# A recurrent attention kernel: token AV in front of memory AV in shared accumulators, side work in one accumulator with ACT casts, the left projection spread over three steps

## The chip, the cores and the metric

The kernel runs on one core of a Trainium2 chip. The core has five engines with queues of their own: TensorE (PE; PEld in the profile is its weight loads), VectorE (DVE), ScalarE (ACT), GpSimd (POOL) and SyncE (SP, which issues DMAs here). They meet only at semaphores. The metric is device time in microseconds (us), lower is better, as the median of several runs.

## The reference

Two branches are mixed by a gate. Branch A is attention over segments of 32 tokens, one after the other, with 8 memory rows that are carried from segment to segment:

```python
for s in range(n_seg):                       # 64 segments of 32 tokens
    h = concat([mem, xs])                    # 8 memory rows + 32 tokens
    q, k, v = h @ Wq, h @ Wk, h @ Wv         # 32 heads of 128
    p = softmax(where(mask, q @ k.T * scale, -1e9))
    o = (p @ v) @ Wo                         # summed over heads
    mem = o[:, :M, :]                        # memory of the next segment
    outs.append(o[:, M:, :])
a = concat(outs)
b = gelu(layernorm(x) @ w1 + b1) @ w2 + b2
return g * a + (1 - g) * b                   # g = sigmoid((x * gate_w).sum(-1))
```

The sequence has 2048 tokens of width 512; everything is bf16. The mask lets every row see the memory, and a token see itself and earlier tokens. Only the memory rows make a recurrence: the outputs of the tokens of a segment are needed by nobody but the result.

## The kernel before

It first computes branch B and the gates (a PE-filled stage of some 100 us), then 64 steps, one per segment, then a tail.

A **step** works on 32 columns: 8 memory rows and the first 24 tokens of the segment. The 8 tokens that are left over in each segment (the "left" part) are projected for four segments at once, one **tile** of 128 tokens ahead, as side work. Wo of the left tokens, and the output rows, are side work too.

In order of TensorE, a step is this (line numbers of the profile). The projections to Q and K fill five PSUM banks (`qk_unit`, L211); DVE transposes each from its bank to SBUF as f32 (`qk_tr`, L217), and ACT, for one bank POOL, casts it to bf16 (L667). V follows in two banks (`v_unit`, L222), cast by ACT. Then come the scores (L383, and L387 for the left keys), Exp on ACT (L685, L686), and the sums of the memory queries by matmul (`sums`, L360). DVE takes their reciprocal (L692) and multiplies (Pm, L695). **Memory AV** (`av`, L398 and L403 with Pm) multiplies V by the probabilities of the 8 memory queries into four banks, one per group j of heads. Four copies bring them to UTT (L703), two on DVE and two on ACT, alternating. The sums of the token queries follow and DVE takes their large reciprocal (L704). Wo over all heads (`wo_unit`, L233) yields the 8 new memory rows and, in the same 32 columns, 24 token rows of an earlier segment. ACT casts the result (wsb, L711). `mask_mm` (L374) writes the mask into the score bank of the next step, the bank that the large reciprocal has read. **Token AV** (`av_x`: `av` with Px, the probabilities of the token queries) follows, for the segment before. `mem_out` (L365) transposes the new memory rows by matmul, and DVE copies them to hT (L721), for which the next step's first matmul waits.

Between these pieces the program pulls **units** of side work out of a generator (`run_fill`, `side_work`): four matmuls of 512 columns each, in most of them. Five units stand in the wait for Pm (six in the fourth step of a tile), one behind the sums, none (two in the fourth step) behind token AV, and what is left of the step's units at the end, behind `mem_out`. The first step of a tile holds 8 units of the left V, the second and third 8 units of left Q and K each, and the fourth two of `out_units` and eight of `wo_left`.

Side work accumulates in two banks, 5 and 6, in turn (`side`). What empties a bank is put into a queue of the program (`later`) and written out at set places: `flush(dve_q)` for transposes and output, `flush(act_q)` for the casts of V and of Wo's left rows. `side` itself flushes when the bank that it needs has not been emptied. POOL casts the transposed left Q and K (L264, L268), copies the left V from a DMA bounce into VL (L299), fills the token columns of hT, and computes Px and a running check sum (L620 to L622).

The order on each engine is the program's order (a manual schedule); waits are set between the pieces where one reads what another wrote or reuses a buffer. PSUM has eight banks: five rotate through the projections and the two AVs (`ring`), 5 and 6 serve the side work, 7 the scores. The tail (L725 to L789) finishes the last two segments, their Wo, and the last two tiles of output; a check of overflow (L796 to L805) follows, with a slow path that is not taken here.

Of the kernel before, what the change touches and what calls it, by code (L numbers as in the profile page):

```python
# [23 lines left out]
def kernel(ctx, tc, A_x, A_mem0, A_Wq, A_Wk, A_Wv, A_Wo, A_seg_len, B_x, B_w1, B_b1, B_w2, B_b2, gate_w, out):  # L24
    nc = tc.nc
    P = 128
# [147 lines left out]

    pools.update(nTt=2, nside=1)

# [17 lines left out]
    def side(shape, dtype=FP32):  # L194
        side_n[0] += 1
        n = pools["nside"]
        while side_n[0] - n in side_todo:
            flush(dve_q)
            flush(act_q)
        return bank(5 + side_n[0] % n, shape, dtype)  # L200

# [51 lines left out]
    def left_qk(T, t, hf):  # L253
        h0, h1 = HF[hf]
        bk = side([P, 512])
        side_k = side_n[0]
        for kc in range(KC):
            qk_unit(bk, GLs[T], t, h0, h1, kc)
            if kc < KC - 1:
                yield  # L260
        def ev():
            Tv = qk_tr(bk, h0, h1)
            if t == 0:
                nc.gpsimd.tensor_copy(out=QL[T % 2][:, h0:h1, :], in_=Tv)  # L264
            else:
                for hh in range(h0 // 8, h1 // 8):
                    r0 = 8 * hh - h0
                    nc.gpsimd.tensor_copy(out=KL[T % 2][:, :, :, hh, :], in_=Tv[:, r0:r0 + 8, :].rearrange("p g (s c) -> p g s c", c=LEFT))  # L268
        later(dve_q, ev, side_k)
        yield  # L270

    def left_v(T, vb):
# [7 lines left out]
        def ev():  # L280
            vt = pools["sb"].tile([P, 4, Dh], BF16, tag="vt", bufs=1, name="vt")
            nc.scalar.copy(out=vt[:].rearrange("p i e -> p (i e)"), in_=bk[:])
            if vb == 0:
                vds[T] = dr.tile([P, 4, 2, Dh], BF16, tag="vd", name="vd")
            nc.sync.dma_start(vds[T][:, 2 * vb:2 * vb + 2], vt[:].rearrange("p (a g) e -> p a g e", g=2))
            if vb == 1:
                src = vds.pop(T)[:].rearrange("(j s c) h g e -> j h c s (g e)", j=4, s=SPT)
                vs = pools["sb"].tile([P, SPT, 2, Dh], BF16, tag="vs", bufs=1, name="vs")
                for j in range(4):
                    for hh in range(4):  # L290
                        r0 = 32 * j + LEFT * hh
                        nc.sync.dma_start(vs[r0:r0 + LEFT].rearrange("p s g e -> p s (g e)"), src[j, hh])
                vls[T] = vs
# [7 lines left out]
    def wo_left(T):  # L301
        bk = side([P, Dm])
        side_k = side_n[0]
        for u in range(8):
            wo_unit(bk, UTT[T % 2], 32, u)
            if u < 7:
                yield

        def ev():
            w = cw.tile([P, Dm], BF16, tag="wsbL", bufs=1, name="wsbL")  # L310
            nc.scalar.copy(out=w[:], in_=bk[:])
            wsbLs[T] = w
        later(act_q, ev, side_k)
        yield

    def out_units(T):
        ob = side([P, Dm])
# [9 lines left out]
        def ev():  # L327
            o_sb = cw.tile([P, Dm], BF16, tag="o", bufs=1, name="o")
            nc.vector.scalar_tensor_tensor(out=o_sb[:], in0=ob[:], scalar=g_all[:, T:T + 1], in1=c_all[:, T, :], op0=ALU.mult, op1=ALU.add)
            nc.sync.dma_start(out2[T * P:(T + 1) * P, :], o_sb[:])  # L330
        later(dve_q, ev, side_k)
        yield

    def side_work(T, si):


        if si < 3 and T + 1 < NT:
            for n in range(2):
                if si == 0:
                    yield from left_v(T + 1, n)  # L340
                else:
                    yield from left_qk(T + 1, n, si - 1)
        if si == 3 and T >= 2:
            yield from out_units(T - 2)
        if si == 3 and T >= 1:
            yield from wo_left(T - 1)

# [43 lines left out]

    def av(U, n, s, V, Pt, c_main, c_left, u0):

        T, si = divmod(s, SPT)
        for i in range(NG):
            for j in range(4):
                q = slice(32 * j, 32 * j + 32)
                nc.tensor.matmul(U[j][:, i, :], lhsT=V[q, i, :], rhs=Pt[q, i, c_main:c_main + n],  # L398
                                 start=(i == 0), stop=False, skip_group_check=True, tile_position=(32 * j, 0))
        for g in range(2):  # L400
# [97 lines left out]
    def setup():  # L498
# [14 lines left out]
        for hf in range(2):  # L513
            for t in range(2):
                for _ in left_qk(0, t, hf):
                    pass
                flush(dve_q)
                yield
# [77 lines left out]
    cw = loop.enter_context(tc.tile_pool(name="cw", bufs=2))  # L596
    pools.update(ps=pb, sb=cw, nTt=3, nside=2)

# [31 lines left out]
    def ux_out(s):  # L630
        T, si = divmod(s, SPT)
        c0 = 24 - 8 * si
        for j, U in enumerate(Uxs.pop(s)):
            nc.scalar.copy(out=UTT[T % 2][:, :, j, c0 + M:c0 + 40], in_=U[:])  # L634

    for s in range(nseg):
# [14 lines left out]
        if s >= 2:  # L651
            ux_out(s - 2)
            flush(act_q)
        if s + 1 < nseg:
# [35 lines left out]
        nc.scalar.copy(out=v_out(V, 1), in_=vb1[:])  # L690
        run_fill(5 + (si == 3))
        nc.vector.reciprocal(out=R[:, 0:8 * NG].rearrange("p (i q) -> p i q", q=8), in_=sm[:])  # L692
        Pm = cw.tile([P, NG, 16], BF16, tag="Pm", bufs=1, name="Pm")
        for c in (8, 0):
            nc.vector.tensor_tensor(out=Pm[:, :, c:c + 8], in0=E[:, :, c:c + 8], in1=R[:, 0:8 * NG].rearrange("p (i q) -> p i q", q=8), op=ALU.mult)  # L695
        Um = [bank(k, [P, NG, 8]) for k in (nd, ne, na, nc_)]
        av(Um, 8, s, V, Pm, 8, 0, 0)
        sr = B[:, 0:NG * 32].rearrange("p (i q) -> p i q", q=32)
# [3 lines left out]
        for j in range(4):  # L702
            (nc.scalar.copy if j % 2 else nc.vector.tensor_copy)(out=UTT[Tp % 2][:, :, j, 24 - 8 * sp:24 - 8 * sp + M], in_=Um[j][:])  # L703
        nc.vector.reciprocal(out=R[:, 8 * NG:].rearrange("p (i q) -> p i q", q=32), in_=sr)  # L704
# [9 lines left out]
        S_next = mask_mm()  # L714
        if s >= 1:
            av_x(s - 1, (nd, ne, na, nc_))
        run_fill(2 * (si == 3))
        if s + 1 < nseg:
# [17 lines left out]
    nc.vector.tensor_tensor(out=Px[:, :, 32:40], in0=E[:, :, 48:56], in1=Rq[:, :, 24:32], op=ALU.mult)  # L736
    nc.gpsimd.tensor_tensor(out=racc[:, 8 * NG:], in0=racc[:, 8 * NG:], in1=Rl, op=ALU.add)
    Es.pop(s), Rs.pop(s)
    Pxs[s] = Px
    for _ in fill:  # L740
        pass
    flush(act_q, 9)

    def wo_x(sw, k, ut, c0):
        wp = bank(k, [P, Dm])
        for u in range(8):
            wo_unit(wp, ut, c0, u)
        wsb = cw.tile([P, Dm], BF16, tag="wsb", bufs=9, name="wsb")
        nc.scalar.copy(out=wsb[:], in_=wp[:])
        wsbs[sw + 2] = wsb  # L750

    U1, U0 = UTT[(NT - 1) % 2], UTT[NT % 2]
    wo_x(s - 2, nb, U1, 16)
    for j, U in enumerate(Uxs.pop(s - 1)):
        (nc.vector.tensor_copy if j % 2 else nc.scalar.copy)(out=U1[:, :, j, 8 + M:48], in_=U[:])
    for _ in out_units(NT - 2):
        flush(dve_q, 9)
    av_x(s, (nd, ne, na, nc_))
    wo_x(s - 1, nb, U1, 8)

# [3 lines left out]
    for j, U in enumerate(Ul):  # L764
        (nc.vector.tensor_copy if j % 2 else nc.scalar.copy)(out=U1[:, :, j, 32:40], in_=U[:, :, RIDE:32])
    wo_x(s, 6, U0, 0)
    T = NT - 1
# [155 lines left out]
```

## Time and profile before

| what | us |
|---|---|
| median of 10 runs (822.4 to 823.99) | 823.18 |
| the profiled execution | 822.21 |
| its span, first to last instruction | 820.4 |
| first matmul of the first step | 100.91 |
| first matmul of the last step | 795.91 |
| DVE busy | 493.2 |
| ACT busy | 446.1 |
| POOL busy | 272.3 |

The granted TensorE clock was 0.999 over the span. Times of rows are microseconds from the span's start, then the duration of the row; a row of the timeline merges several instructions of one kind (x32). In brackets stands how long the engine was idle before the row, and what ended that. The busy time of PE counts matmuls by modelled ends, so a busy PE may still wait. The lines themselves stand with the prediction.

### The profile page before, as it was taken

The page shows a single profiled execution, that of the slowest core. Times are in us where ns is not written, and L with a number is a line of the kernel's source. Part 1 is how long each engine was busy: PE and PEld are TensorE (multiplying, and loading weights), DVE is VectorE, ACT ScalarE, POOL GpSimd, SP SyncE. Part 2 cuts the span into 40 slices and gives each one's busy share as a digit, 9 for nine tenths or more (in the row PEclk, how much of TensorE's full clock was granted, in tenths as well). Part 3 has the DMA queues.
Part 4 walks back from the last instruction along what each step waited for, and adds up shares of the span by engine and source line. Part 5 has one row for each costly group of instructions (what it writes and reads, how often), then busy time and mean ns, then how long its engine had stood idle before and what let it go on. Part 6 is the DMA issues. An engine that isn't in the chain of part 4 may idle for free.

```text
span 820.4 us, 48425 instructions
## 1 busy us (share of the span) xinstructions
PE 792.5 (97%) x22001; PEld 444.2 (54%) x22013; DVE 493.2 (60%) x1022; ACT 446.1 (54%) x1239; POOL 272.3 (33%) x624
## 2 busy tenths in 40 slices
PE   6999999999999999999999999999999999999986
PEld 3666545555555555555555555555555555555543
DVE  5764256565656666665666565666566565756554
ACT  3555445555555555555555645555564555565553
POOL 8100224242434243243424242433333242424220
PEclk9999999999999999999999999999999999999999
DMA  8791300000000010101010100001010101010000
GB/s 305 245 405 51 104 28 12 25 16 17 24 20 26 13 34 10 37 11 35 5 38 9 31 16 21 25 18 28 10 36 11 36 4 40 7 33 8 10 5 24
DMA packets 38357, 37.59 MB, mean 46 GB/s; under 512 B 13561, under 2 KB 36578, under 8 KB 36610
## 3 DMA queue, kind: packets, MB, share of 16 engines
q1 hardware_dynamic: 38018, 34.31, 12.6%
q8 instruction: 174, 2.85, 1.4%
q0 software_dynamic: 128, 0.13, 0.1%
q14 instruction: 37, 0.30, 0.1%
HBM read 26.03 MB, written 6.29 MB: 39 GB/s over the span
## 4 chain that ended last, share of the span: by engine, by line
PE 93%; DVE 3%; DMA 1%; issue 1%; SPq 1%; ACT 1%; DVEq 0%; ACTq 0%
PE b L211 34%; PE b L233 18%; PE b L222 16%; PE b L398 5%; PE hp L470 4%; PE bp L487 4%; PE b L360 3%; PE b L374 2%; PE b L383 2%; PE b L365 2%; PE b L403 1%; DMA Wo_sb<-in_A_x_dram 1%; PE b L387 0%; DVE hT L721 0%; DVE Tt L217 0%
## 5 line engine op out<-in xcount | busy, mean ns | idle before, releaser
L217 DVE STREAM_TRANSPOSE Tt<-b 128x512 f32<-128x512 f32 (+1 forms) x384 | 225.7, 613 | 82.1 <-PE b L211 70.3
L211 PEld LDWEIGHTS <-hT 128*32 128x32 bf16 x5120 | 131.6, 97 | 108.1 <-DVE hT L721 23.9
L233 PE MATMUL b<-Wo_sb,UTT 128*32 128x512 bf16 (+1 forms) x2656 | 160.9, 378 | 1.3 <-ACT UTT L763 0.9
L222 PE MATMUL b<-Wv_sb,hT 128*32 128x512 bf16 x2048 | 141.9, 379 | 0.0
L211 PE MATMUL b<-Wq_sb,hT 128*32 128x512 bf16 x2048 | 133.4, 380 | 3.2 <-DVE hT L721 1.7
L211 PE MATMUL b<-Wk_sb,hT 128*32 128x256 bf16 (+1 forms) x3072 | 133.4, 308 | 0.0
L667 ACT CAST KT<-Tt 128x256 bf16<-128x256 f32 (+1 forms) x192 | 87.1, 476 | 53.6 <-DVE Tt L217 53.5
L620 POOL TENSOR_TENSOR Px<-E,R 128x256 bf16<-128x256 bf16 x63 | 42.4, 674 | 209.1 <-DVE R L704 209.1
L704 DVE RECIPROCAL R<-b 128x256 f32<-128x256 f32 x63 | 110.7, 1757 | 0.0
L667 POOL CAST QT<-Tt 128x512 bf16<-128x512 f32 x64 | 39.1, 611 | 187.2 <-DVE Tt L217 187.2
L233 PEld LDWEIGHTS <-UTT 128*32 128x32 bf16 x2656 | 64.6, 96 | 63.6 <-DVE UTT L703 12.1
L711 ACT CAST wsb<-b 128x512 bf16<-128x512 f32 x63 | 36.9, 585 | 111.2 <-PE b L233 111.2
L692 DVE RECIPROCAL R<-b 128x64 f32<-128x64 f32 x63 | 35.1, 557 | 78.5 <-PE b L360 78.5
L634 ACT CAST UTT<-b 128x256 bf16<-128x256 f32 x248 | 74.4, 387 | 9.9 <-PE b L403 7.6
L667 ACT CAST QT<-Tt 128x512 bf16<-128x512 f32 x64 | 39.6, 619 | 68.3 <-DVE Tt L217 68.3
L222 PEld LDWEIGHTS <-hT 128*32 128x32 bf16 x2048 | 49.6, 96 | 21.1
L475 ACT ACTIVATE hg<-hp,b_sb 128x256 bf16<-128x256 f32 x80 | 37.8, 473 | 40.3 <-PE hp L470 40.3
L398 PEld LDWEIGHTS <-V 32*128 32x128 bf16 x4064 | 34.5, 91 | 45.5 <-DVE Pm L695 32.2
L721 DVE CAST hT<-b 128x32 bf16<-128x32 f32 x63 | 12.1, 192 | 78.1 <-PE b L365 78.1
L470 PE MATMUL hp<-yT,w_sb 128*128 128x256 bf16 (+1 forms) x352 | 54.9, 282 | 2.3 <-DMA w_sb<-in_B_w_dram 1.1
L703 ACT CAST UTT<-b 128x64 bf16<-128x64 f32 x126 | 20.6, 215 | 66.1 <-PE b L403 66.1
L622 POOL TENSOR_TENSOR racc<-racc,R 128x320 f32<-128x320 f32 x63 | 54.7, 868 | 0.0
(131 smaller groups left out, 1053.9 us busy)
## 6 DMA issues: line engine op xcount, KB each, us to landing
Wv_sb<-in_A_Wv_dram SPq DMA_DIRECT2D x4, 1024.0 KB
Wq_sb<-in_A_Wq_dram SPq DMA_DIRECT2D x4, 1024.0 KB
Wk_sb<-in_A_Wk_dram SPq DMA_DIRECT2D x4, 1024.0 KB
Wo_sb<-in_A_Wo_dram SPq DMA_DIRECT2D x2, 2048.0 KB
vd<-vt SPq DMA_DIRECT2D x32, 128.0 KB
vs<-vd SPq DMA_DIRECT2D x256, 16.0 KB
out_dram<-o SPq DMA_DIRECT2D x15, 128.0 KB
Wo_sb<-in_A_x_dram SPq DMA_DIRECT2D x1, 1024.0 KB
```

Of the source, the lines that this page charges most:

```text
L211: nc.tensor.matmul(bk[32 * j:32 * j + 32, 0:n], lhsT=G[:, kc, :], rhs=W5[t][:, kc, h0:h1, j, :], start=(kc == 0), stop=(kc == KC - 1), til ...
L217: nc.vector.transpose(out=Tt[:, 0:n], in_=bk[:, 0:n])
L222: nc.tensor.matmul(bk[32 * j:32 * j + 32, :], lhsT=G[:, kc, :], rhs=Wv5[:, kc, 4 * vb:4 * vb + 4, j, :], start=(kc == 0), stop=(kc == KC - ...
L233: nc.tensor.matmul(bk[32 * g:32 * g + 32, :], lhsT=ut[:, i, j, c0:c0 + 32], rhs=Wo_sb[:, 4 * i + j, d0:d1], start=(j == 0 and i < 4), stop ...
L398: nc.tensor.matmul(U[j][:, i, :], lhsT=V[q, i, :], rhs=Pt[q, i, c_main:c_main + n], start=(i == 0), stop=False, skip_group_check=True, til ...
L470: nc.tensor.matmul(hp[:rows, :], lhsT=w1_sb[:, kc, fc * P:fc * P + rows], rhs=yTs[blk][:, kc, :], start=(kc == 0), stop=(kc == KC - 1))
L475: nc.scalar.activation(out=hg_[:rows, :], in_=hp[:rows, :], func=ACTF.Gelu_apprx_tanh, bias=b1_sb[:rows, fc:fc + 1], scale=1.0)
L620: nc.gpsimd.tensor_tensor(out=Px[:, :, 0:32], in0=E[:, :, 16:48], in1=Rr, op=ALU.mult)
L622: nc.gpsimd.tensor_tensor(out=racc[:], in0=racc[:], in1=R[:], op=ALU.add)
L634: nc.scalar.copy(out=UTT[T % 2][:, :, j, c0 + M:c0 + 40], in_=U[:])
L667: (nc.gpsimd.tensor_copy if bi == 2 else nc.scalar.copy)(out=dst, in_=Tv)
L704: nc.vector.reciprocal(out=R[:, 8 * NG:].rearrange("p (i q) -> p i q", q=32), in_=sr)
```

## The change

Token AV of the segment before moves in front of memory AV. Both now write one accumulator per group of heads: 320 columns, of which memory AV takes the first 64; only the first matmul of token AV opens the bank, and memory AV adds into it without opening it again. The four UTT copies of the memory rows are all on ACT.

Side work that goes through `side` has bank 5 alone. Its banks are emptied by ACT: left Q and K are cast to bf16 (`lt`) and then transposed by DVE in SBUF straight into QL and KL, with no POOL cast; the output rows are scaled by ACT (into a buffer of the transposes' ring, `of`), and POOL adds the other branch. `wo_left` has bank 6 for itself: it begins with one unit in the second step and one in the third, and the other six stand in the fourth. The steps of a tile thus hold 8, 9, 9 and 8 units. Three units stand in the wait for Pm (four in the first step of all), one behind the sums, two behind `mask_mm` (three in the second and third step), the rest at the end. ACT's queue is flushed at the start of every step, not from the third on. In the tail, the check sum's addition moves from POOL to DVE and further back, the casts of wsb are taken out of `wo_x`, and the output rows of the last tile but one move behind the last Wo of 512 columns.

```diff
-pools.update(nTt=2, nside=1)
+pools["nTt"] = 2
...
     side_n[0] += 1
-    n = pools["nside"]
-    while side_n[0] - n in side_todo:
-        flush(dve_q)
+    while side_n[0] - 1 in side_todo:
         flush(act_q)
-    return bank(5 + side_n[0] % n, shape, dtype)
+    return bank(5, shape, dtype)
...
     def ev():
-        Tv = qk_tr(bk, h0, h1)
-        if t == 0:
-            nc.gpsimd.tensor_copy(out=QL[T % 2][:, h0:h1, :], in_=Tv)
-        else:
-            for hh in range(h0 // 8, h1 // 8):
-                r0 = 8 * hh - h0
-                nc.gpsimd.tensor_copy(out=KL[T % 2][:, :, :, hh, :], in_=Tv[:, r0:r0 + 8, :].rearrange("p g (s c) -> p g s c", c=LEFT))
-    later(dve_q, ev, side_k)
+        lt = pools["sb"].tile([P, 512], BF16, tag="lt", name="lt")
+        nc.scalar.copy(out=lt[:], in_=bk[:])
+        def tr():
+            if t == 0:
+                nc.vector.transpose(out=QL[T % 2][:, h0:h1, :].rearrange("p h r -> p (h r)"), in_=lt[:])
+            else:
+                for hh in range(h0 // 8, h1 // 8):
+                    r0 = 32 * (8 * hh - h0)
+                    nc.vector.transpose(out=KL[T % 2][:, :, :, hh, :],
+                                        in_=lt[:, r0:r0 + 256].rearrange("p (g s c) -> p g s c", s=SPT, c=LEFT))
+        dve_q.append((None, tr))
+    later(act_q, ev, side_k)
     yield
...
     def ev():
-        vt = pools["sb"].tile([P, 4, Dh], BF16, tag="vt", bufs=1, name="vt")
+        vt = pools["sb"].tile([P, 4, Dh], BF16, tag="lt", name="vt")
         nc.scalar.copy(out=vt[:].rearrange("p i e -> p (i e)"), in_=bk[:])
...
 def wo_left(T):
-    bk = side([P, Dm])
-    side_k = side_n[0]
+    bk = bank(6, [P, Dm])
     for u in range(8):
...
         wsbLs[T] = w
-    later(act_q, ev, side_k)
+    act_q.append((None, ev))
     yield
-def out_units(T):
+def out_units(T, last=False):
     ob = side([P, Dm])
...
         o_sb = cw.tile([P, Dm], BF16, tag="o", bufs=1, name="o")
-        nc.vector.scalar_tensor_tensor(out=o_sb[:], in0=ob[:], scalar=g_all[:, T:T + 1], in1=c_all[:, T, :], op0=ALU.mult, op1=ALU.add)
+        if last:
+            nc.vector.scalar_tensor_tensor(out=o_sb[:], in0=ob[:], scalar=g_all[:, T:T + 1], in1=c_all[:, T, :], op0=ALU.mult, op1=ALU.add)
+        else:
+            of = cw.tile([P, Dm], FP32, tag="Tt", bufs=pools["nTt"], name="of")
+            nc.scalar.activation(out=of[:], in_=ob[:], func=ACTF.Copy, scale=g_all[:, T:T + 1])
+            nc.gpsimd.tensor_tensor(out=o_sb[:], in0=of[:], in1=c_all[:, T, :], op=ALU.add)
         nc.sync.dma_start(out2[T * P:(T + 1) * P, :], o_sb[:])
-    later(dve_q, ev, side_k)
+    later(act_q, ev, side_k)
     yield
+wls = {}
 def side_work(T, si):
-    if si < 3 and T + 1 < NT:
+    if si < 3:
         for n in range(2):
-            if si == 0:
-                yield from left_v(T + 1, n)
-            else:
-                yield from left_qk(T + 1, n, si - 1)
-    if si == 3 and T >= 2:
-        yield from out_units(T - 2)
-    if si == 3 and T >= 1:
-        yield from wo_left(T - 1)
+            if T + 1 < NT:
+                yield from left_v(T + 1, n) if si == 0 else left_qk(T + 1, n, si - 1)
+            if n == 0 and si > 0 and T >= 1:
+                if si == 1:
+                    wls[T - 1] = wo_left(T - 1)
+                next(wls[T - 1])
+                yield
+    if si == 3:
+        if T >= 2:
+            yield from out_units(T - 2)
+        if T >= 1:
+            yield from wls.pop(T - 1)
...
-def av(U, n, s, V, Pt, c_main, c_left, u0):
+def av(U, n, s, V, Pt, c_main, c_left, u0, first=True):
...
             nc.tensor.matmul(U[j][:, i, :], lhsT=V[q, i, :], rhs=Pt[q, i, c_main:c_main + n],
-                             start=(i == 0), stop=False, skip_group_check=True, tile_position=(32 * j, 0))
+                             start=(first and i == 0), stop=False, skip_group_check=True, tile_position=(32 * j, 0))
     for g in range(2):
...
                 pass
+            flush(act_q)
             flush(dve_q)
...
 cw = loop.enter_context(tc.tile_pool(name="cw", bufs=2))
-pools.update(ps=pb, sb=cw, nTt=3, nside=2)
+pools.update(ps=pb, sb=cw, nTt=3)
...
     for j, U in enumerate(Uxs.pop(s)):
-        nc.scalar.copy(out=UTT[T % 2][:, :, j, c0 + M:c0 + 40], in_=U[:])
+        nc.scalar.copy(out=UTT[T % 2][:, :, j, c0 + M:c0 + 40], in_=U)
...
         ux_out(s - 2)
-        flush(act_q)
+    flush(act_q)
     if s + 1 < nseg:
...
     nc.scalar.copy(out=v_out(V, 1), in_=vb1[:])
-    run_fill(5 + (si == 3))
+    run_fill(3 + (s == 0))
     nc.vector.reciprocal(out=R[:, 0:8 * NG].rearrange("p (i q) -> p i q", q=8), in_=sm[:])
...
         nc.vector.tensor_tensor(out=Pm[:, :, c:c + 8], in0=E[:, :, c:c + 8], in1=R[:, 0:8 * NG].rearrange("p (i q) -> p i q", q=8), op=ALU.mult)
-    Um = [bank(k, [P, NG, 8]) for k in (nd, ne, na, nc_)]
-    av(Um, 8, s, V, Pm, 8, 0, 0)
+    U4 = [bank(k, [P, NG * 40]) for k in (nd, ne, na, nc_)]
+    Um = [u[:, 0:NG * 8].rearrange("p (i q) -> p i q", q=8) for u in U4]
+    if s >= 1:
+        Ux = [u[:, NG * 8:].rearrange("p (i q) -> p i q", q=32) for u in U4]
+        av(Ux, 32, s - 1, Vs.pop(s - 1), Pxs.pop(s - 1), 0, 32, 24)
+        Uxs[s - 1] = Ux
+    av(Um, 8, s, V, Pm, 8, 0, 0, first=(s == 0))
     sr = B[:, 0:NG * 32].rearrange("p (i q) -> p i q", q=32)
...
     for j in range(4):
-        (nc.scalar.copy if j % 2 else nc.vector.tensor_copy)(out=UTT[Tp % 2][:, :, j, 24 - 8 * sp:24 - 8 * sp + M], in_=Um[j][:])
+        nc.scalar.copy(out=UTT[Tp % 2][:, :, j, 24 - 8 * sp:24 - 8 * sp + M], in_=Um[j])
     nc.vector.reciprocal(out=R[:, 8 * NG:].rearrange("p (i q) -> p i q", q=32), in_=sr)
...
     S_next = mask_mm()
-    if s >= 1:
-        av_x(s - 1, (nd, ne, na, nc_))
-    run_fill(2 * (si == 3))
+    run_fill(2 + (1 <= si <= 2))
     if s + 1 < nseg:
...
 nc.vector.tensor_tensor(out=Px[:, :, 32:40], in0=E[:, :, 48:56], in1=Rq[:, :, 24:32], op=ALU.mult)
-nc.gpsimd.tensor_tensor(out=racc[:, 8 * NG:], in0=racc[:, 8 * NG:], in1=Rl, op=ALU.add)
 Es.pop(s), Rs.pop(s)
 Pxs[s] = Px
-for _ in fill:
-    pass
-flush(act_q, 9)
...
         wo_unit(wp, ut, c0, u)
+    return sw, wp
+def wo_x_out(sw, wp):
     wsb = cw.tile([P, Dm], BF16, tag="wsb", bufs=9, name="wsb")
...
 U1, U0 = UTT[(NT - 1) % 2], UTT[NT % 2]
-wo_x(s - 2, nb, U1, 16)
+w61 = wo_x(s - 2, nb, U1, 16)
 for j, U in enumerate(Uxs.pop(s - 1)):
     (nc.vector.tensor_copy if j % 2 else nc.scalar.copy)(out=U1[:, :, j, 8 + M:48], in_=U[:])
-for _ in out_units(NT - 2):
-    flush(dve_q, 9)
+wo_x_out(*w61)
+for _ in fill:
+    pass
+flush(act_q, 9)
 av_x(s, (nd, ne, na, nc_))
-wo_x(s - 1, nb, U1, 8)
+w62 = wo_x(s - 1, nb, U1, 8)
...
     (nc.vector.tensor_copy if j % 2 else nc.scalar.copy)(out=U1[:, :, j, 32:40], in_=U[:, :, RIDE:32])
-wo_x(s, 6, U0, 0)
+nc.vector.tensor_tensor(out=racc[:, 8 * NG:], in0=racc[:, 8 * NG:], in1=Rl, op=ALU.add)
+wo_x_out(*w62)
+w63 = wo_x(s, 6, U0, 0)
+wo_x_out(*w63)
+for _ in out_units(NT - 2, True):
+    pass
+flush(act_q, 9)
 T = NT - 1
```

## What is predicted, and why

> **What bounds the kernel now.** First the page's shares and its chain that ended last:
>
> ```profile
> PE 792.5 (97%) x22001; PEld 444.2 (54%) x22013; DVE 493.2 (60%) x1022; ACT 446.1 (54%) x1239; POOL 272.3 (33%) x624
> PE 93%; DVE 3%; DMA 1%; issue 1%; SPq 1%; ACT 1%; DVEq 0%; ACTq 0%
> ```
>
> Both say TensorE. The sums over stretches, cut at the first query matmul of a step, say otherwise:
>
> ```profile
> core 0: us, PE busy (x) PEld busy (x) DVE busy (x) ACT busy (x) POOL busy (x), PEclk, DMA share, GB/s
> 454.35:465.18 10.83, 10.83 (x333) 5.92 (x333) 6.59 (x13) 6.40 (x19) 2.59 (x7) 1.00 0.09 30
> 465.18:475.95 10.77, 10.77 (x336) 5.91 (x332) 6.05 (x13) 6.35 (x19) 2.98 (x7) 1.00 0.15 42
> 520.54:531.48 10.94, 10.90 (x336) 5.91 (x332) 7.57 (x15) 5.75 (x18) 5.49 (x12) 1.00 0.06 14
> 531.48:542.92 11.44, 11.33 (x344) 6.23 (x340) 7.33 (x15) 6.21 (x20) 4.69 (x10) 1.00 0.02 4
> 763.57:774.39 10.82, 9.41 (x300) 5.35 (x301) 6.60 (x13) 5.91 (x18) 2.59 (x7) 1.00 0.04 15
> 774.39:785.15 10.76, 9.35 (x301) 5.35 (x301) 6.01 (x12) 5.87 (x18) 2.98 (x7) 1.00 0.02 5
> ```
>
> These are the first, second, third and fourth step of a tile (10.83, 10.77, 10.94, 11.44, together 43.98), then two steps of the last tile, which have no side units at all. Without side units PE is busy 1.4 us less and the step takes the same time. A step is bounded by its own chain of waits; units are free while they fit into the waits. The timeline of the second step without units shows that chain:
>
> ```profile
> 779.94 0.24 PE L360 MATMUL b<-E,BO 128*32 128x64 bf16 x8
> 780.23 0.56 DVE L692 RECIPROCAL R<-b 128x64 f32<-128x64 f32 x1 [1.62 <-PE b L360]
> 780.89 0.36 DVE L695 TENSOR_TENSOR Pm<-E,R 128x64 bf16<-128x64 bf16 x2
> 781.17 0.36 PE L398 MATMUL b<-Pm,V 32*128 32x8 bf16 x32 [0.99 <-DVE Pm L695]
> 781.68 0.36 DVE L703 CAST UTT<-b 128x64 bf16<-128x64 f32 x2 [0.43 <-PE b L403]
> 781.72 0.33 ACT L703 CAST UTT<-b 128x64 bf16<-128x64 f32 x2 [0.94 <-PE b L403]
> 781.96 1.91 PE L233 MATMUL b<-Wo_sb,UTT 128*32 128x512 bf16 x32
> 782.00 1.76 DVE L704 RECIPROCAL R<-b 128x256 f32<-128x256 f32 x1
> 783.81 0.37 PE L374 MATMUL b<-MkA,ident 128*32 128x448 bf16 x4
> 783.92 0.58 ACT L711 CAST wsb<-b 128x512 bf16<-128x512 f32 x1 [1.88 <-PE b L233]
> 784.56 0.27 PE L365 MATMUL b<-Sel,wsb 128*32 128x8 bf16 x16
> 784.90 0.19 DVE L721 CAST hT<-b 128x32 bf16<-128x32 f32 x1 [1.15 <-PE b L365]
> 785.15 1.05 PE L211 MATMUL b<-Wq_sb,hT 128*32 128x512 bf16 x16 [0.32 <-DVE hT L721]
> ```
>
> Start to start: projections to sums (774.39 to 779.94) 5.55; sums to memory AV 1.23 (reciprocal and Pm); to Wo 0.79 (UTT copies); to wsb 1.96; to mem_out 0.64; to hT 0.34; to the next step 0.25. That is the floor, 10.76.
>
> **What the steps lose now.** One unit is 0.216 us (four banks' starts in steps with units, 410.22 to 413.69, are 16 units). The fourth step has six units in the Pm wait: sums at 404.38, memory AV at 405.85, 1.47 instead of 1.23; and two behind token AV, so wsb to mem_out is 1.01 instead of 0.64. That is 0.61 of its 0.68 over the floor. In the third step Pm takes 0.59 instead of 0.36, beside POOL's 1.04 us VL copy (437.75), and memory AV comes 0.13 late. The rest, 0.05 to 0.06 in all but the second step, is a two-semaphore wait at the third QK transpose, which starts at +2.90 instead of +2.82.
>
> **The change, part by part.** Memory AV is the AV of 8 queries, token AV that of 32.
>
> Pm wait. New: sums 0.06, three units 0.65, the turn to row tiles 0.11 (end of the sixth unit to memory AV in the fourth step), token AV 0.26, together 1.08 of 1.23. Token AV gets a new wait: its fourth accumulator is the bank of the sums, which the reciprocal reads until +0.85 (0.29+0.56), with about 0.06 for the semaphore. Behind that matmul in PE's queue stand the rest of token AV (0.19 and 0.05) and memory AV, and behind this the whole chain: 0.91+0.24=1.15, still before Pm at 1.23. Price 0. The ends: token AV as a whole behind the reciprocal with 0.45 (784.11 to 784.56, its start to the next work's) is 1.36, +0.13 a step; below, memory AV now waits at the matmul instead of at its weight load, at most -0.05. I take 0, since the order of the queue is known. The fourth step saves 0.24. POOL has no casts of the left part any more, so its VL copy follows the QT cast (3.68+0.61=4.29 into the step) and with GL and hT (0.29, 0.27) is over by 5.9, before Pm at 6.5: the third step saves 0.13.
>
> Side by side the two AVs save one turn to row tiles (0.11) and one back (0.13 in the fourth step: token AV's last eight matmuls at 409.00 take 0.05, the next unit starts at 409.18). I count them as nothing: both lie in waits that end elsewhere. Here the Trainium skill has a rule: TensorEngine Tiling (Array Packing), Key Properties, says that a change of tiling mode drains the array, so by it every turn less would be a gain, 15 us over 62 steps; the equal times of steps with and without units speak against it.
>
> UTT copies all on ACT. Two copies of 0.215 take 0.33 there, so starts are 0.11 apart; ACT starts 0.03 behind DVE. Wo needs the quarters in order j, each for two units (0.43): now Wo starts 0.05 after the first DVE copy and before the last, so it waits quarter by quarter. First quarter +0.015; the fourth is over 0.3 later than the first but is not needed for 1.3. Ends: -0.01 and +0.34 (all four waited for); I take +0.015, 1 us in all.
>
> The skill speaks against this part: the same page, PSUM Bottleneck, wants both ScalarE and VectorE on PSUM evacuation. By it all four copies would count, +0.34 a step or 21 us; the rows of Wo's start are nearer.
>
> DVE without UTT copies starts the large reciprocal up to 0.08 earlier; mask_mm waits for it (1.76) and gets free at about Wo's end. Gain 0, as wsb is what ends this stretch.
>
> wsb wait. From Wo's end, 1.73 after its start, to mem_out there are 0.87. Mask 0.19 and two units 0.43 fit; three units (second and third step) make 0.84, a tie: 0.02 each. Ends 0 and 0.22 a unit. Token AV has left, and the fourth step saves 0.37. Two units behind mem_out cover the hT copy as before.
>
> Side work on ACT. Each left bank now costs a cast of 0.62 (as vt) instead of an f32 transpose and a POOL cast. The first of a step stands between the UTT copies and wsb, where ACT idles 1.88; 0.22+0.62 fit. The second stands behind the token copies (1.20), which start 0.3 earlier since their data is old; today vt stands there and the QT cast behind it still finds 0.69 idle. The next unit in bank 5 comes 1 us after the cast. The out scaling takes that first place in the fourth step. Price 0; cover gone, up to 0.62 each in 45 steps.
>
> bf16 transposes on DVE have no row. f32 from PSUM takes 0.72; DVE idles 1.2 before the first QK transpose and 1.6 before the small reciprocal: 0, and +0.3 a step if they take twice as long. The out addition on POOL is between 0.67 (x256) and 1.74 (racc's 0.87 doubled); behind it in the queue are hT, the QT copy and Px, all needed 4 us later: 0. Its output DMA leaves SP half a step earlier, with only the next tile's vd behind it. DMA bytes are unchanged. The third transpose's double wait leaves two of three steps: 0.05 each.
>
> A tile comes to 10.80+10.81+10.81+10.78=43.20 instead of 43.98: 0.78 in tiles 2 to 14, 10.1; tile 1, whose fourth step is 11.26, 0.6.
>
> First two steps. In the second a left transpose stands before the small reciprocal (118.80, 0.72, the reciprocal only at 119.44 instead of 117.87); flushing ACT's queue in every step removes that: 12.24 to 10.79, -1.45. In the first, four units finish a bank in the Pm wait, so the fifth waits for UTT copies and vt on ACT: Wo at about +1.9 instead of +0.86 behind memory AV, +1.0. The preparation gets four casts (2.5) between gelus with 0.40 idle each: 0 to 1, taken as 0.
>
> Tail. Today:
>
> ```profile
> 807.28 0.40 PE L320 MATMUL b<-wsb,SelX 128*32 128x512 bf16 x4 [1.19 <-DVE bad L804]
> 809.10 0.75 DVE L329 SCALAR_TENSOR_TENSOR o<-b,g_all,c_all 128x512 bf16<-128x512 f32 x1 [1.82 <-DMA out_dram<-o]
> 811.03 3.66 PE L233 MATMUL b<-Wo_sb,UTT 128*32 128x512 bf16 x96 [0.91 <-ACT UTT L763]
> ```
>
> The new order takes away 1.19 and 0.91; the last output then waits about 0.9 for the DMA of the one before (one o buffer, 1.82 today). Net -1.2, between -2.5 and +0.5.
>
> Sum: -10.7-0.45-1.2=-12.4. The profiled execution took 822.21 (span 820.4 and 1.8 around it), so 809.8; it stands 0.97 below the median of 823.18, so **810.8**.
>
> **Rivals.**
> The saved turns count (7%): 0.24 more a step, 62 times, 15 us, about 796. Against it: equal steps with and without units.
> Token AV late (11%): +0.1 in 61 steps, 817. For it the new wait in a full queue.
> The third unit isn't hidden (10%): +0.2 in 28 steps, 816. For it the tie of 0.84 and 0.87.
> Slower (8%): Wo starts behind all four ACT copies, +0.34 in 62 steps, 831. It decides from 0.20 a step on (12.4/62). Against it the start of Wo before the last copy today.
> No change (4%): longer waits give back all.
>
> **How the numbers follow.** The forecast has 60%; its own range is 807.5 to 813.5. 806 to 818 takes in the two milder rivals and the ends of tail and ties and leaves out the saved turns, the slower rival and the rest. Faster 0.87 (forecast, saved turns, token AV, third unit), same 0.04, slower 0.09; within 0.2% a measurement of this kernel can't tell a change.
>
> **What would show it.** Steps of 10.8 in all four places; sums to memory AV 1.23 with token AV inside; Wo 0.80 behind memory AV; mask no longer after the large reciprocal; Pm 0.36 in the third step; the second step of all near 10.8. Wrong if memory AV comes later than 1.3 behind the sums, if Wo is over 0.9 behind it, or if mem_out is over 0.7 behind wsb.

## The result and the profile after

The changed kernel takes 819.53 us (median of 9 runs, 818.18 to 821.73) beside 823.21 us of before (822.22 to 824.27): a ratio of 0.9958, 95% interval 0.9949 to 0.9966. It is faster, by 3.7 us where 12.4 had been predicted, and outside the predicted range of 806 to 818. The profiled execution took 821.65 us, span 819.8; it lies 2.1 over the median of its kernel, so that in the two profiled executions only 0.56 us of the gain is to be seen.

The page after, its shares and its chain that ended last:

```profile
PE 783.8 (96%) x22001; PEld 442.2 (54%) x22013; DVE 459.9 (56%) x915; ACT 496.6 (61%) x1443; POOL 243.9 (30%) x541
PE 92%; DVE 2%; ACT 2%; issue 1%; DMA 1%; SPq 1%; DVEq 0%; ACTq 0%
```

The work has gone from DVE and POOL to ACT as described, and the chain is TensorE's as before. What has become of the steps is in the sums over stretches: a first, second, third and fourth step of a tile, then one more second and one more fourth step, then two steps of the last tile, which have nearly no side units. The columns are the stretch, its length, the busy time of PE, PEld, DVE, ACT and POOL with their instructions, then the granted clock, the DMA share and GB/s:

```profile
454.00:464.76 10.76, 10.76 (x337) 5.89 (x334) 5.68 (x10) 6.88 (x22) 2.52 (x6) 1.00 0.06 18
201.41:212.27 10.86, 10.86 (x341) 6.08 (x338) 5.76 (x11) 7.10 (x23) 2.65 (x6) 1.00 0.18 48
212.27:223.12 10.85, 10.85 (x340) 6.07 (x336) 6.95 (x14) 6.98 (x23) 4.14 (x9) 1.00 0.03 7
707.92:718.66 10.74, 10.74 (x336) 5.86 (x332) 6.91 (x13) 7.04 (x22) 2.83 (x5) 1.00 0.03 8
244.82:256.49 11.67, 10.88 (x340) 5.96 (x337) 5.75 (x11) 6.98 (x22) 3.46 (x7) 1.00 0.16 44
442.01:454.00 11.99, 10.81 (x336) 5.85 (x333) 6.92 (x13) 6.93 (x22) 4.39 (x8) 1.00 0.05 16
762.92:773.67 10.75, 9.43 (x304) 5.41 (x300) 5.68 (x10) 6.38 (x21) 3.03 (x7) 1.00 0.01 3
773.67:784.43 10.76, 9.65 (x304) 5.34 (x304) 5.69 (x10) 5.97 (x20) 3.01 (x7) 1.00 0.02 5
```

The first four are within 0.05 of what was predicted: 10.76, 10.86, 10.85, 10.74, together 43.21 (predicted 43.20, before 43.98), and the last two, 10.75 and 10.76 with 1.1 to 1.3 us less of PE's work, show that it is the floor. The two between (a second and a fourth step) have nearly the same busy time of PE, PEld, DVE and ACT, but are 0.81 and 1.25 longer: time in which PE is idle. POOL is busy 0.8 and 1.6 more in them, with one and three instructions more inside the cuts. Such steps come irregularly. Taking from every step between 188 and 763 us (52 of them) the fastest of its place in the tile, 2.06 us are left over in before, and 11.52 us after; 19 of the 52 steps are more than 0.15 us over the fastest.

So the tiles' gain is there (0.78 in each of 13 tiles, 10.1 us) and is paid back by 9.5 us of pauses.

**Where a pause stands.** The timeline of one such step (from 244.82), around the two AVs:

```profile
251.19 0.44 PE L410 MATMUL b<-Px,V 32*128 32x32 bf16 x32
251.60 0.37 PE L410 MATMUL b<-Pm,V 32*128 32x8 bf16 x32
251.97 0.32 PE L372 MATMUL b<-E,BO 128*32 128x256 bf16 x8
252.11 0.56 ACT L722 CAST UTT<-b 128x64 bf16<-128x64 f32 x4 [0.90 <-PE b L415]
252.12 0.39 PE L209 MATMUL b<-Wq_sb,GL 128*32 128x512 bf16 x4
252.60 0.58 ACT L261 CAST lt<-b 128x512 bf16<-128x512 f32 x1
253.30 1.48 PE L231 MATMUL b<-Wo_sb,UTT 128*32 128x512 bf16 x23 [0.79 <-ACT lt L261]
```

and of the undisturbed first step from 454.00:

```profile
460.37 0.45 PE L410 MATMUL b<-Px,V 32*128 32x32 bf16 x32
460.80 0.36 PE L410 MATMUL b<-Pm,V 32*128 32x8 bf16 x32
461.17 0.32 PE L372 MATMUL b<-E,BO 128*32 128x256 bf16 x8
461.31 0.56 ACT L722 CAST UTT<-b 128x64 bf16<-128x64 f32 x4 [0.92 <-PE b L415]
461.32 0.39 PE L220 MATMUL b<-Wv_sb,GL 128*32 128x512 bf16 x4
461.57 1.70 PE L231 MATMUL b<-Wo_sb,UTT 128*32 128x512 bf16 x28
```

From the UTT copies to Wo there are 0.26 us in the one and 1.19 in the other. The copies took 0.56 in both. The releaser that the profile names in the first, ACT's cast of the left part into lt, misleads: Wo reads no lt, and the cast merely was the last thing to happen before PE went on. In other steps the same kind of pause stands inside memory AV, inside Wo, at the sums of the token columns, or at a unit of the side work. So no single producer is late.

**What the pauses have in common** is their number in PE's queue. The page has a row that stands in before and after alike:

```profile
q8 instruction: 174, 2.85, 1.4%
```

174 packets of 16384 bytes. They go with TensorE's 44,000 loads and matmuls, one for each 256 of them, a **block**. With loads and matmuls counted through from the first load, 22 pauses over 0.2 us in the kernel after end at instructions whose numbers leave the same remainder when divided by 256. They are 14.8 us together, what would have been waited for anyway included, and 18 of the 19 late steps have one of them. (Not counted, here and below, are gaps at that remainder that end more than 1.7 us after the block's packet has landed, since there something else is waited for: five after. The traces of before and after lack 12 matmul records ahead of the loop, 22001 beside 22013 loads; the runs below have all, and their remainder is 12 higher.) Four of those boundaries after, and one before, from the list of packets; the position counts from the first load of the step's projections:

| step from | position in the step | packet starts | landed | PE ahead of it | PE behind it | landed to start |
|---|---|---|---|---|---|---|
| after 244.82 | 529, Wo | 250.66 | 251.84 | 252.13 | 253.30 | 1.46 |
| after 354.39 | 497, memory AV | 359.70 | 361.08 | 361.40 | 362.34 | 1.27 |
| after 442.01 | 529, Wo | 448.36 | 449.24 | 449.32 | 450.81 | 1.57 |
| after 454.00 | 377, token AV | 456.43 | 457.50 | 460.54 | 460.54 | 3.04 |
| before 244.71 | 529, Wo | 251.14 | 252.02 | 253.83 | 253.83 | 1.81 |

No instruction behind a boundary starts earlier than 1.2 us after its packet has landed: the least is 1.22 in after, and 1.19 to 1.31 in each of the ten traces of this document. After's 22 pauses end 1.22 to 1.57 after the landing. With some 1.04 us for the packet itself (median), a block can be used about 2.3 us after its packet starts. PE pauses where it gets through what it has in less: at the 22 pauses it had 160 to 228 instructions ahead of the boundary left when the packet started. How fast it does is seen in the densest 2.4 us of a step, PE and PEld together; before, then after:

```profile
459.11:461.51 2.40, 2.40 (x100) 1.28 (x96) 0.92 (x3) 1.68 (x6) 0.40 (x1) 1.00 0.00 0
```

```profile
458.78:461.18 2.40, 2.40 (x135) 1.50 (x132) 0.92 (x3) 1.61 (x6) 0.40 (x1) 1.00 0.00 0
```

196 instructions in before, 267 after: the 160 of the two AVs go by in 0.8 us and now stand in one place. Before, token AV came 2.9 us after memory AV, behind Wo's 64 long instructions.

That also explains the rhythm. Five steps have 3336 or 3344 instructions, 13 blocks and 8 or 16, so a boundary comes back to nearly the same position every fifth step: the steps from 244.82, 299.74, 354.39 pause at positions 529, 513, 497, and the one from 409.50 at 489 only by 0.10. All 22 lie at positions 465 to 585, and each of the 15 boundaries at 497 to 553 has a pause.

### The profile page after: what moved, and what is told of

The parts are those of the page before. It is cut to its first block, busy times and chain, and to the rows that moved or that the text cites. A ratio compares the mean times of both kernels' runs of the same rounds, so it can differ in the third digit from the quotient of the medians.

```text
span 819.8 us, 48304 instructions
## 1 busy us (share of the span) xinstructions
PE 783.8 (96%) x22001; PEld 442.2 (54%) x22013; DVE 459.9 (56%) x915; ACT 496.6 (61%) x1443; POOL 243.9 (30%) x541
## 4 chain that ended last, share of the span: by engine, by line
PE 92%; DVE 2%; ACT 2%; issue 1%; DMA 1%; SPq 1%; DVEq 0%; ACTq 0%
PE b L209 34%; PE b L231 17%; PE b L220 16%; PE b L410 5%; PE hp L482 4%; PE bp L499 4%; PE b L372 3%; PE b L386 2%; PE b L395 2%; PE b L377 1%; PE b L415 1%; DMA Wo_sb<-in_A_x_dram 1%; ACT wsb L730 1%; PE b L399 0%; PE b L326 0%
## 5 line engine op out<-in xcount | busy, mean ns | idle before, releaser
L215 DVE STREAM_TRANSPOSE Tt<-b 128x512 f32<-128x512 f32 (+1 forms) x320 | 180.9, 596 | 75.5 <-PE b L209 62.2
L231 PE MATMUL b<-Wo_sb,UTT 128*32 128x512 bf16 (+1 forms) x2656 | 168.2, 378 | 3.7 <-ACT of L335 1.1
L220 PE MATMUL b<-Wv_sb,hT 128*32 128x512 bf16 x2048 | 140.2, 379 | 0.0
L722 ACT CAST UTT<-b 128x64 bf16<-128x64 f32 x252 | 35.3, 227 | 60.7 <-PE b L415 60.7
L410 PEld LDWEIGHTS <-V 32*128 32x128 bf16 x4064 | 44.1, 91 | 30.7 <-issue 29.9
L487 ACT ACTIVATE hg<-hp,b_sb 128x256 bf16<-128x256 f32 x80 | 37.7, 473 | 34.5 <-PE hp L482 34.5
```

Source lines behind the costliest of these rows:

```text
L215: nc.vector.transpose(out=Tt[:, 0:n], in_=bk[:, 0:n])
L220: nc.tensor.matmul(bk[32 * j:32 * j + 32, :], lhsT=G[:, kc, :], rhs=Wv5[:, kc, 4 * vb:4 * vb + 4, j, :], start=(kc == 0), stop=(kc == KC - ...
L231: nc.tensor.matmul(bk[32 * g:32 * g + 32, :], lhsT=ut[:, i, j, c0:c0 + 32], rhs=Wo_sb[:, 4 * i + j, d0:d1], start=(j == 0 and i < 4), stop ...
```

## The experiments

The theory (called block theory) is that PE waits for its own instructions to be brought. Rivals: ACT, which now makes all copies and casts, is late now and then; or the shared accumulators make token or memory AV wait.

**One block boundary in every step, at a chosen place.** Idle matmuls (pads) between the projection banks bring each step to 768 instructions, three blocks; the number of them in the first step sets where the boundaries fall in all the others.

```diff
+    def extra(n):
+        for _ in range(n):
+            for j in range(4):
+                q = slice(32 * j, 32 * j + 32)
+                nc.tensor.matmul(B[q, 480:481], lhsT=ident[:, q], rhs=ident[:, 0:1], start=False, stop=True,
+                                 skip_group_check=True, tile_position=(0, 32 * j))
...
             (nc.gpsimd.tensor_copy if bi == 2 else nc.scalar.copy)(out=dst, in_=Tv)
+            if bi < 4:
+                extra((EXTRA[s] + bi) // 4)
```

EXTRA holds the groups of a step: 13, 12, 12, 13 in a tile, more in the first and the last tiles, whose steps are shorter. In the first step it is 17, 33 or 9 in the three kernels.

> In the trace of after, 22 pauses of TensorE of 0.2 to 1.5 us end at instructions whose numbers leave the same remainder when divided by 256; 256 instructions are what one 16384-byte packet of the instruction queue brings, and no such instruction runs earlier than 1.22 us after its packet has landed. They lie 460 to 581 instructions into a step, behind the two AVs. This kernel is after with idle one-column matmuls between the projection banks (12 to 21 groups of four a step, none of them read), so that every step has 768 instructions = 3 blocks, and 17 such groups in the first step, so that one block boundary falls about 525 instructions (the pads not counted) into every step. Block theory: all of some 60 steps pause, by about 0.6 to 1.2 us each, and this kernel is 30 to 60 us slower than its twin with the boundary elsewhere. Rival (ACT, which now makes all UTT copies and the left casts, is late now and then) and rival (the shared accumulators wait): pads in the projections change nothing there, and both twins take the same time within 2 us. The pads themselves cost both twins up to 0.9 us a step (52 pairs at the 0.017 us of mem_out's pairs), some 55 us.

> The same kernel with 33 groups of pads in the first step instead of 17, nothing else: the block boundaries fall at about 141, 397 and 653 instructions (the pads not counted) into every step. Block theory: no pause behind the AVs in any step, all steps of a place alike within 0.05 us, and 30 to 60 us less than its twin. Rivals: as irregular as after, and the time of the twin within 2 us (1 us more for the 64 extra pairs).

> The padded kernel a third time, with 9 idle groups in the first step (17 and 33 in the twins run before): every block boundary lies 64 instructions later in its step than in the slower twin, which paused in all 62 steps; the boundaries fall at about 345 and 601 instructions (pads not counted), ahead of token AV and behind Wo's middle, where after never paused by more than 0.1 us. Block theory: almost no pauses behind the AVs, steps of a place alike (11.0 to 11.2 by the fastest steps of the twins), 828 to 840. If the twins differ for another reason (number of pads in the first step): near the slower twin, 870 to 878, as it is nearer to it in pads.

Measured: 877.83 us (ratio to before 1.0673, 1.0657 to 1.069), 847.24 (1.0284, 1.0265 to 1.0303) and 840.15 (1.0219, 1.0199 to 1.0239). The boundary in question stood at 529, 401 and 337 with the pads left out in steps of 13 groups, and 8 later in steps of 12. Kernels with the same steps, which differ by 16 or 8 groups of idle matmuls in one step of 64, differ by 30.6 and 37.7 us, and the one with most pads is not the slowest. The profiled executions of the first two, both at a granted clock of 0.995, differ by 28.4. In the first, PE pauses at the boundary in each of 62 steps (63 pauses over 0.2 us in all, 60.0 us with what would have been waited for anyway). A tile of it, then of the third:

```profile
432.79:444.57 11.78, 11.09 (x388) 6.21 (x384) 5.80 (x10) 6.94 (x22) 3.25 (x7) 1.00 0.07 20
444.57:456.14 11.57, 11.23 (x389) 6.21 (x385) 5.86 (x11) 7.05 (x22) 2.98 (x6) 1.00 0.15 41
456.14:467.65 11.51, 11.22 (x388) 6.23 (x384) 7.07 (x14) 7.05 (x22) 4.15 (x8) 1.00 0.03 9
467.65:479.65 12.00, 11.13 (x388) 6.19 (x384) 7.02 (x13) 7.10 (x22) 3.77 (x7) 1.00 0.05 16
```

```profile
370.98:382.00 11.02, 11.02 (x388) 6.19 (x384) 5.80 (x10) 6.95 (x22) 3.72 (x9) 1.00 0.09 27
382.00:393.16 11.16, 11.16 (x388) 6.33 (x384) 5.85 (x11) 7.16 (x23) 3.10 (x7) 1.00 0.17 45
393.16:404.32 11.16, 11.16 (x389) 6.44 (x385) 7.07 (x14) 7.05 (x23) 4.16 (x9) 1.00 0.04 9
404.32:415.38 11.06, 11.06 (x388) 6.13 (x385) 7.01 (x13) 6.98 (x22) 3.18 (x6) 1.00 0.03 8
```

The same counts of PE's instructions and nearly the same work, 46.86 us beside 44.40. Two expectations were missed, both for the clean case: the second kernel was to have no pause behind the AVs, and the third to take at most 840. The pads make the stretch ahead of token AV denser too, so the second kernel still has 42 pauses (18.4 us), 22 of them inside token AV. The third has 49 (24.0 us), of which 34 fall at or just behind the mask, where PE waits for the large reciprocal anyway; its steps are only 7.3 us over the fastest of their place, in 52 steps. The rivals expected the same time within 2 us for the first two kernels, and the third near the slower one; they are out as the cause of these pauses.

**The UTT copies back on both engines.**

```diff
-            nc.scalar.copy(out=UTT[Tp % 2][:, :, j, 24 - 8 * sp:24 - 8 * sp + M], in_=Um[j])
+            (nc.scalar.copy if j % 2 else nc.vector.tensor_copy)(out=UTT[Tp % 2][:, :, j, 24 - 8 * sp:24 - 8 * sp + M], in_=Um[j])
```

> After with the four UTT copies of memory AV alternating between VectorE and ScalarE, as before, nothing else. Block theory: the pauses stay (some 20, together about 10 us); time within 2 us of after's 819.5. Rival (ACT is the cause): the pauses go, about 811.

822.13 us, ratio 0.9988 (0.9979 to 0.9997): 2.6 us more than after, where at most 2 had been expected. The pauses stay, 21 of them, 14.8 us. A step without and one with:

```profile
575.60:586.36 10.76, 10.76 (x338) 5.85 (x334) 7.22 (x15) 6.71 (x20) 3.40 (x7) 1.00 0.05 16
608.06:619.86 11.80, 11.02 (x340) 6.14 (x336) 7.31 (x16) 6.84 (x21) 4.14 (x9) 1.00 0.04 10
```

So ACT's load isn't the cause, and the copies on one engine are no loss. The Trainium skill (TensorEngine Tiling (Array Packing), PSUM Bottleneck), weighed in the prediction, advises both engines; here both engines were 2.6 us slower than one. Of these the trace shows 0.04 a tile (43.24 beside 43.20 for the fastest steps); where the rest lies stays open, since the profiled executions differ by 0.2 us in span only.

**The order alone, on before.** Token AV in front in shared accumulators, three units ahead of it, two or three behind the mask; casts, copies, left Wo and tail as in before.

```diff
-        run_fill(5 + (si == 3))
+        run_fill(3)
...
+            av(Ux, 32, s - 1, Vs.pop(s - 1), Pxs.pop(s - 1), 0, 32, 24)
...
+        av(Um, 8, s, V, Pm, 8, 0, 0, first=(s == 0))
...
-            av_x(s - 1, (nd, ne, na, nc_))
-        run_fill(2 * (si == 3))
+        run_fill(2 + (si == 3))
```

> Before with the order alone: token AV in front of memory AV in shared accumulators, three units ahead of it and two (three in the fourth step) behind the mask; the left part keeps its VectorE transposes and POOL casts in two banks, the UTT copies alternate, left Wo stays in the fourth step, the tail is before's. Block theory: the pauses come with the order, 20 to 30 of them at one remainder of 256 and 10 to 16 us in all; time 819 to 825. Rival (ScalarE's new work or the flush of its queue makes the pauses): none, steps regular as in before, 813 to 816.

825.74 us, ratio 1.0023 (1.0013 to 1.0033): slower than before, just over the upper end that was expected. A fourth step without a pause and a first step with one:

```profile
488.68:499.74 11.06, 11.06 (x345) 6.28 (x345) 7.48 (x15) 5.96 (x19) 4.50 (x10) 1.00 0.01 4
499.74:511.23 11.49, 10.86 (x336) 6.07 (x328) 6.45 (x13) 6.64 (x19) 3.19 (x7) 1.00 0.09 27
```

The fastest steps of a tile sum to 43.55 beside 43.98, a gain of 5.6 us over 13 tiles; 20 pauses at one remainder (15.0 us) take it back and more. The order brings the pauses, without any of ACT's new work.

**All but the order.** After with token AV back behind the mask, so that Wo's long matmuls stand between the AVs; side work in two banks in turn, so that five units fit into the Pm wait, and left Wo as seven units in a fourth step and one in the next (units 9, 8, 8, 9).

```diff
-        run_fill(3 + (s == 0))
+        run_fill(5)
+        flush(act_q, 1 if si == 0 and T >= 2 else 0)
...
-            av(Ux, 32, s - 1, Vs.pop(s - 1), Pxs.pop(s - 1), 0, 32, 24)
...
         S_next = mask_mm()
-        run_fill(2 + (1 <= si <= 2))
+        if s >= 1:
+            av_x(s - 1, (nd, ne, na, nc_))
+        run_fill(T >= 2 and si in (0, 3))
```

> After with token AV back behind the mask in accumulators of its own, so that 64 units' worth of 512-column matmuls lie between the two AVs again; casts, copies, flushes and tail as in after; side work in two banks in turn, five units in the Pm wait, left Wo as seven units in the fourth step and one in the next (a tile's units 9, 8, 8, 9). Block theory: at most 192 instructions in 2.4 us as before, almost no pauses; steps 10.75 to 10.9 in all four places, 809 to 814. Rival (ACT): irregular pauses as in after, 818 to 821. If only token AV's place counts as cover: the fifth unit and token AV behind wsb cost 0.2 a step, about 822.

811.94 us, ratio 0.986 (0.9845 to 0.9875): faster than both kernels. A tile:

```profile
406.40:417.35 10.95, 10.95 (x341) 6.05 (x338) 5.68 (x10) 6.97 (x23) 3.74 (x8) 1.00 0.07 20
417.35:428.11 10.76, 10.76 (x336) 5.89 (x332) 5.75 (x11) 6.91 (x22) 2.80 (x7) 1.00 0.17 47
428.11:438.88 10.77, 10.77 (x336) 5.91 (x332) 6.97 (x14) 6.99 (x22) 4.16 (x9) 1.00 0.03 8
438.88:449.84 10.96, 10.96 (x341) 6.05 (x338) 6.92 (x13) 7.33 (x23) 3.50 (x7) 1.00 0.05 16
```

Between the AVs stand Wo's 64 instructions, which are 8 units (the expectation says 64 units). The fastest steps sum to 43.43, 0.23 more than after's 43.20, as the ninth unit shares the wsb wait with token AV (0.81 instead of 0.64). But there is one pause over 0.2 us (0.47) in the whole loop, and the 52 steps are 1.5 us over the fastest instead of 11.5.

**The tail.** The last output tile in a buffer of its own, and the count of bad sums in another bank, on after; then the buffer alone on the kernel just shown.

```diff
-    o_sb = cw.tile([P, Dm], BF16, tag="o", bufs=1, name="o")
+    o_sb = cw.tile([P, Dm], BF16, tag="lt", name="o")
...
-    cnt = side([1, 1])
+    cnt = bank(7, [1, 1])
```

> After with the last output tile in a buffer of its own (that of the left part, free by then) and the count in the bank of the scores; nothing else. The tail theory: in after the last scaling waits 1.42 us for the output transfer ahead of it and the count's result comes behind it, so that the tail keeps 24.6 us although its TensorE part is over 1.2 us earlier; both gone give 1.3 to 3.3 us: 816.2 to 818.2. If the end is set by something else: 819.5.

> The kernel with token AV back behind the mask (units 9, 8, 8, 9) and the last output tile in a buffer of its own. The last scaling waited 1.34 us there: 810.6 to 811.2 instead of 811.9. If the end is set elsewhere: 811.9.

On after: 819.08 us, ratio 0.9954 (0.994 to 0.9967), not to be told from after's 0.9958 and over the expected 816.2 to 818.2. The profile shows why something was to be had, first of after, then of this kernel:

```profile
809.66 0.75 DVE L332 SCALAR_TENSOR_TENSOR o<-b,g_all,c_all 128x512 bf16<-128x512 f32 x1 [0.96 <-PE b L326]
813.25 0.88 DVE L812 SCALAR_TENSOR_TENSOR o<-b,g_all,c_all 128x256 bf16<-128x256 f32 x2 [1.42 <-DMA out_dram<-o]
814.04 0.13 DVE L828 TENSOR_SCALAR bad<-b 1x1 int32<-1x1 f32 x1
```

```profile
808.72 0.75 DVE L332 SCALAR_TENSOR_TENSOR o<-b,g_all,c_all 128x512 bf16<-128x512 f32 x1 [0.95 <-PE b L326]
810.81 0.96 DVE L812 SCALAR_TENSOR_TENSOR o<-b,g_all,c_all 128x256 bf16<-128x256 f32 x2
811.69 0.13 DVE L828 TENSOR_SCALAR bad<-b 1x1 int32<-1x1 f32 x1
```

The wait of 1.42 is gone, and from the last step's start to the end of the span there are 22.9 us instead of 24.6. In the medians 23 pauses (14.2 us) of varying length drown it. The new bank did not bring the count forward; it still runs behind the last scaling. On the kernel with the AVs apart the buffer alone gives 810.72 us, ratio 0.985 (0.9835 to 0.9866), runs of 810.4 to 811.4: the fastest kernel here, as expected, although its interval overlaps that of the one before. There the AVs apart do the work; the 1.2 us of the tail are within what the two intervals allow.

## Why the prediction was wrong, point by point

- **A step is bounded by its own chain, floor 10.76: right.** Undisturbed steps after are 10.76, 10.86, 10.85, 10.74. The saved turns of the rival, 0.24 a step, are not to be seen in them.
- **Token AV costs nothing in the Pm wait: right as to its waits, wrong as a whole.** From the sums to memory AV there are 1.23 to 1.25 us in every step after, as in the undisturbed steps before. The new wait on the sums' reader is to be seen in the last tile alone, where no units precede it, and is over before Pm is. But "Price 0" was worked out from waits and durations only. This is the step of the prediction that failed: the sum lets TensorE run through 160 short instructions, 16 for the sums and Wo at the pace of the rows, as if it always had them at hand. The runs show that a block boundary inside or close behind this stretch costs up to 1.5 us of PE time (at positions 497 to 553 always, 0.2 us at least): 9.5 us over 52 steps, three quarters of the predicted 12.4. None of the rivals had it, so the range couldn't hold it.
- **Could it have been seen?** The parts were in the trace of before: the queue's row, one packet of 1.04 us for 256 instructions, a boundary (position 529 from 244.71) at which PE came 1.81 us after the landing, 0.6 more than the least, and two small pauses (0.11 and 0.31 us) of the same kind. Nobody had counted how many instructions the new order puts into one stretch.
- **UTT copies all on ACT, +0.015 a step: right and a little better.** Wo follows memory AV by 0.77 to 0.78 (0.80 predicted).
- **Fourth step and third step: right.** 10.74 and 10.85 instead of 11.44 and 10.94; the VL copy no longer delays Pm.
- **The third unit, 0.02: too small.** From wsb to mem_out there are 0.73 instead of 0.64, over the 0.7 that the prediction named as a sign of being wrong, and 0.03 more to hT: 0.10 to 0.12 in two of four steps. The first and fourth steps were 0.04 better than predicted, so a tile's sum came out right by luck.
- **First two steps, -0.45: measured -0.13.** The first is 11.79 (11.18 before, +0.61 instead of +1.0); the second is 11.49 instead of 10.79, for a pause of 0.78 us at a boundary. With the AVs apart the two take 21.47 instead of 23.28.
- **Tail, -1.2: measured +0.14.** From the last step's start to the last scaling it is 18.08 instead of 19.24, -1.16 as predicted, though with luck: the wait for the DMA in it is 1.42, where 0.9 was put. What was left out: the count (L828) now stands behind the last scaling on DVE, at 814.04, where it had stood at 807.14 in before, and from the last scaling's start to the end of the span there are 6.55 us instead of 5.25. In the kernels with the AVs apart, where the count runs early, it is 4.6 and 5.6, and 6.3 in the tail run on after, where it still runs last. That the count is what ends the program fits this, but no run moved it alone, and the three kernels in which it runs early differ by 1.0 among themselves, so the cause of the longer end stays open.
- **Start.** The first step begins 0.40 later (0 to 1 had been allowed, 0 taken).
- **Chances.** Forecast, saved turns, token AV and third unit add up to 0.88 for faster, not 0.87.

In the profiled executions these make 0.40 - 0.13 - 1.00 (steps 3 to 63) + 0.14 = -0.6.

## What to carry to other kernels

Count instructions, not only durations: where short matmuls are brought together, compare the most instructions in some 2.4 us of a step with what the kernel had before, and look whether the new pauses of an engine share a remainder in its instruction numbers. A wait whose named releaser writes nothing that the waiting instruction reads is a sign of it. Filling the waits of a chain was worth nearly the same in two orders here (43.20 and 43.43 us a tile without pauses); take the one that keeps long matmuls between short ones: units in the Pm wait and token AV behind the mask gave 811.9 us, the opposite 819.5.

## What the runs showed of the hardware that had not been expected

TensorE's instructions come in blocks of 256, one packet of 16384 bytes each (median 1.04 us in after), and the first of a block starts no earlier than 1.2 us after the packet landed. At up to 196 instructions in 2.4 us this cost 0.4 us in a whole run (before), at 267 some 10 (after). The Trainium skill (Runtime: NRT & Kernel Launch, Instruction fetch mechanics) describes these refills in 256 instructions and calls the crossing of a block mostly hidden, because an engine issues slower than the refill brings. The runs agree with the first and not with the second: boundary by boundary it cost 0.2 to 1.5 us in and behind the AVs, 22 times in one run and 63 times where every step had one there. Where a boundary falls is decided by the number of all instructions ahead of it, so that eight more idle groups of four in one step made 38 us of difference at the end. After's runs spread over 3.5 us, those of the kernel with the AVs apart over 0.9, which fits pauses that vary with the packets (0.88 to 1.48 us each).
